# 1248 unused bytes ahead of a second stage's row tiles, with its weight tiles left in place

## The chip, the cores and the metric

The kernel runs on one core of one Trainium2 chip. The metric is the device time of one execution in microseconds (us), the median of several runs; a profiled execution gives the trace from which the rows below are read.

## The reference

The input x has 8 x 3072 rows of 256 float32 numbers. Three steps follow one another; the first two make the kernel's first stage, the last one its second stage.

```python
Y = rfft(x, axis=1) * (filt_r + 1j * filt_i)          # a filter along the 3072 rows
x = irfft(Y, n=3072, axis=1).reshape(24576, 256)
x = maximum(maximum(x @ w1, x @ w2), x @ w3) @ w_out   # 256 -> 768 -> 256
h = x @ w_in2                                          # 256 -> 1024
solu = h * softmax(h)
ln = (solu - mean(solu)) / sqrt(var(solu) + 1e-6) * g_ln
out = ln @ w_out2                                      # 1024 -> 256
```

## The kernel before

Every float32 matrix product is split: an operand is written as a high part and a low part of type float32r (`xh`, `xl`; `wi_h`, `wi_l`), and three of the four products are summed in PSUM.

The first stage holds the filter and the first pair of matrix products. Its matmuls are those of `up` (L713), `down` (L733 to L742) and of the transform (L390). It writes its result to DRAM (`spill`), 512 rows at a time.

The second stage treats 192 tiles of 128 rows. `load2` (L877) brings four tiles from `spill` into `x` and splits them into `xh` and `xl`. `up2` (L886) runs 12 matmuls of 512 columns for each tile: a slice of 128 columns of `xh` or `xl` is the stationary operand, and `wi_h` or `wi_l` moves. `soft` (L902) makes the row maximum (VectorE, L905), the exponential (ScalarE, L907), the product (VectorE, L909), the squares (ScalarE, L911), a few numbers per row in `sm` (VectorE, GpSimd) and a transpose in blocks of 32 into `yt` (VectorE, L926). `exchange` (L929) finishes the transpose of four tiles with 16 DMAs from `yt` to `zt`, issued on SP's queue (L935). `split2` (L948) makes `sh` (ScalarE, L959) and `sl` (GpSimd, L960) from `zt`. `down2` (L963) runs 8 matmuls of 512 columns with `sh` as the stationary operand (L967) and 8 of 256 columns with `sl` (L969); `V2` moves in both. So a tile is 28 matmuls and 20 x 512 + 8 x 256 = 12288 moved columns. The loop at L1018 issues `up2` of tile i, `split2` of tile i - 8 and `down2` of tile i - 9; a planner that runs when the program is built settles the order on each engine. The last four tiles are transposed on TensorE (L945).

In SBUF a pool's buffers lie one behind another in the order in which they are first named, and pools that are opened later lie behind those still open. The waits for memory that another pool used before are made against whole pools. The buffers stand at these byte positions in each partition (a second figure is the second buffer):

```
second stage, weights (pool bp):    wi_h 18432   wi_l 26624   V2 34816
second stage, rows (pool b2):       sh 51200, 55296   x 59392, 63488   xh 67584, 71680
                                    xl 75776, 79872   sl 83968, 88064   (pool ends 92160)
second stage, rows (pools b3, b4):  sm 92160   e 92672   sp 100864   yt 109056, 141824
                                    zt 125440, 158208   oa 174592   ob 176640   (ends 178688)
first stage: df 17376   F 71648   M1 75744   M2 79840   U 101344   yt 118752   zt 122848
             xh 155616   xl 163808   hh and th 176096   hl and tl 182240
             w0h 188384   w0l 200672   ah 212960   woh 217056   wol 223200
```

Pool bp already has a gap of 800 bytes ahead of `wi_h`. All the second stage's large buffers named here start at a multiple of 512 bytes, `wi_h`, `V2`, `sh`, `x`, `xh`, `xl` and `sl` at a multiple of 2048. The first stage's start at 480 bytes past a multiple of 512, thus at 224 past a multiple of 256; its `xh`, `hh`, `hl` and its weights stand 2016 bytes past a multiple of 2048. So in both stages a stationary operand and the operand that moves over it start equally far past a multiple of 512 (only `ones` and `ident`, used in a few float32 matmuls, differ).

The slots of `x` and `xh` also serve `weights2` (L842), which makes the second stage's weights during the last 36 of the first stage's 288 steps, and those of `sh` hold `gw` there.

Of the kernel before, what the change touches and what calls it, by code (L numbers as in the profile page):

```python
# [10 lines left out]
F32 = mybir.dt.float32  # L11
# [8 lines left out]
P = 128  # L20
# [79 lines left out]
def kernel(ctx: ExitStack, tc: tile.TileContext, xr, ff, tw, dft,  # L100
# [727 lines left out]
    wi_l = bp.tile([P, 2, DF2], F32R, tag="wil", name="wil")  # L828
    V2 = bp.tile([P, NF2, 512], F32R, tag="V2", name="V2")
    b2 = ctx.enter_context(tc.tile_pool(name="b2", bufs=2))  # L830
    gwt = [b2.tile([P, 4, D], F32, tag="sh", name=f"gw{j}") for j in range(NF2 // 4)]
    gw = [gwt[c // 4][:, c % 4] for c in range(NF2)]

# [263 lines left out]
```

## Time and profile before

| | |
|---|---|
| median of 3 runs | 2739.02 us (2738.84 to 2740.20) |
| profiled execution, its own time | 2739.05 us |
| profiled execution, span of its instructions | 2737.3 us |
| mean granted clock of TensorE | 0.991 of full speed |
| TensorE busy | 2663.2 us (97%) |
| VectorE, ScalarE, GpSimd busy | 2310.0, 1476.7, 887.6 us |

Times in the rows are microseconds from the start of the span, or nanoseconds where a row gives a mean of one instruction. PE is TensorE's matmuls, PEld its loads of stationary operands, DVE VectorE, ACT ScalarE, POOL GpSimd and SP the SyncE queue. Matmuls overlap in the pipeline, so the length given for one matmul is longer than the distance to the next.

### The profile page before, as it was taken

Reading aid. Unit: us, or ns where it says so; the run is one execution under the profiler, and the core shown is the slowest. Engines: PE = TensorE matmul, PEld = TensorE weight load, DVE = VectorE, ACT = ScalarE, POOL = GpSimd, SP = SyncE. Lnnn points to the kernel's source line nnn. Section 1 sums busy time; section 2 is a strip of 40 time slices with the busy share of each in tenths; the row PEclk is TensorE's granted clock in tenths of the full one; section 3 lists DMA queues with packets and bytes.
Section 4 is the critical chain, followed back from the end, with each engine's and each line's share of the span. In section 5 each row is a group of like instructions: output and inputs, shape, how many; then the busy total and the mean of one; then the engine's idle time right before and its main releaser. Section 6 shows DMA issues by size and latency. Waiting matters only on the chain.

```text
span 2737.3 us, 37911 instructions
## 1 busy us (share of the span) xinstructions
PE 2663.2 (97%) x11992; PEld 2146.3 (78%) x11992; DVE 2310.0 (84%) x4023; ACT 1476.7 (54%) x2883; POOL 887.6 (32%) x1286
## 2 busy tenths in 40 slices
PE   6789999999999999999999999999999999999999
PEld 3467777777777777777777888888888888888888
DVE  8997799999998999999977446888787878788885
ACT  4334444444444444443444335777777777777775
POOL 0000010111101111110102003677767666667765
PEclk9889999999999999999999999999999999999999
DMA  4222123224223223232224112555555555555543
GB/s 165 74 81 94 38 80 104 62 75 127 58 72 117 73 71 111 74 93 69 79 66 125 40 30 81 154 139 146 147 143 144 148 148 141 139 141 144 145 127 90
DMA packets 160745, 284.53 MB, mean 104 GB/s; under 512 B 33952, under 2 KB 93856, under 8 KB 158624
## 3 DMA queue, kind: packets, MB, share of 16 engines
q1 hardware_dynamic: 119840, 231.77, 31.8%
q10 hardware_dynamic: 40704, 50.35, 5.6%
q8 instruction: 94, 1.54, 0.2%
q14 instruction: 107, 0.88, 0.1%
HBM read 89.04 MB, written 50.33 MB: 51 GB/s over the span
## 4 chain that ended last, share of the span: by engine, by line
PE 82%; DVE 13%; DMA 2%; issue 1%; SPq 1%; ACT 1%; POOL 0%; DVEq 0%; ACTq 0%; POOLq 0%
PE h L713 22%; PE h L898 19%; PE p L967 13%; PE p L969 7%; PE pf L390 5%; PE o L742 4%; PE o L734 4%; PE o L735 4%; PE o L733 4%; DVE scr L240 3%; DVE S L244 2%; DVE S L240 1%; DVE M L240 1%; DVE h L718 1%; DVE hl L722 1%
## 5 line engine op out<-in xcount | busy, mean ns | idle before, releaser
L960 POOL TENSOR_TENSOR sl<-zt,sh 128x1024 fp32r<-128x1024 f32 x188 | 452.5, 2407 | 106.2 <-ACT sh L959 99.1
L967 PE MATMUL p<-V,sh 128*128 128x512 f32 x1536 | 380.9, 389 | 0.0
L909 DVE SCALAR_TENSOR_TENSOR sp<-h,e 128x1024 f32<-128x1024 f32 x192 | 234.3, 1220 | 171.8 <-ACT e L907 169.8
L240 POOL TENSOR_TENSOR M<-M,M 128x384 f32<-128x384 f32 (+1 forms) x96 | 135.1, 1428 | 655.1 <-DVE M L240 530.5
L967 PEld LDWEIGHTS p<-V,sh 128*128 128x128 f32 x1536 | 287.4, 188 | 59.5
L721 ACT CAST hh<-h 128x512 fp32r<-128x512 f32 x288 | 169.4, 589 | 286.6 <-DVE h L718 272.7
L716 ACT ACTIVATE hm<-h 128x512 f32<-128x512 f32 x288 | 173.0, 601 | 277.6 <-PE h L713 275.5
L907 ACT ACTIVATE e<-h,sm 128x1024 f32<-128x1024 f32 x192 | 213.7, 1113 | 107.1 <-DVE sm L905 61.2
L959 ACT CAST sh<-zt 128x1024 fp32r<-128x1024 f32 x188 | 196.6, 1047 | 117.9 <-PE p L967 94.9
L905 DVE TENSOR_REDUCE sm<-h 128x1 f32<-128x1024 f32 x192 | 231.1, 1204 | 28.0 <-PE h L898 27.3
L911 ACT ACTIVATE e<-sp,sm 128x1024 f32<-128x1024 f32 x192 | 220.5, 1148 | 55.3 <-DVE sm L913 54.2
L734 PE MATMUL o<-hl,woh 128*128 128x512 f32 x576 | 239.4, 416 | 6.1 <-DVE hl L722 5.9
L898 PE MATMUL h<-wih,x2h 128*128 128x512 f32 x768 | 243.9, 392 | 1.2 <-ACT xo L745 1.2
L898 PE MATMUL h<-wih,x2l 128*128 128x512 f32 x768 | 241.8, 391 | 0.0
L718 DVE TENSOR_TENSOR h<-hm,h 128x512 f32<-128x512 f32 x288 | 198.3, 688 | 49.2 <-PE h L713 46.3
L898 PE MATMUL h<-wil,x2h 128*128 128x512 f32 x768 | 238.0, 390 | 0.0
L926 DVE STREAM_TRANSPOSE yt<-sp 128x1024 f32<-128x1024 f32 x188 | 231.6, 1232 | 5.2 <-DMA zt<-yt 1.0
L733 PE MATMUL o<-hh,woh 128*128 128x512 f32 x576 | 230.7, 400 | 2.9 <-ACT hh L721 2.9
L735 PE MATMUL o<-hh,wol 128*128 128x512 f32 x576 | 228.9, 397 | 0.0
L722 DVE TENSOR_TENSOR hl<-h,hh 128x512 fp32r<-128x512 f32 x288 | 196.7, 684 | 36.4 <-ACT hh L721 36.2
L969 PEld LDWEIGHTS p<-V,sl 128*128 128x128 f32 x1536 | 209.7, 190 | 15.1
L969 PE MATMUL p<-V,sl 128*128 128x256 f32 x1536 | 214.7, 282 | 0.0
(160 smaller groups left out, 5722.3 us busy)
## 6 DMA issues: line engine op xcount, KB each, us to landing
zt<-yt SPq DMA_DIRECT2D x752, 128.0 KB, 2.6
x<-xo SPq DMA_DIRECT2D x96, 256.0 KB, 2.2
x<-x ACTq DMA_DIRECT2D x48, 512.0 KB, 3.6
out_dram<-ob ACTq DMA_DIRECT2D x192, 128.0 KB, 2.3
S<-in_xr_dram SPq DMA_DIRECT2D x15, 1536.0 KB, 7.5
zt<-yt SPq DMA_DIRECT2D x720, 32.0 KB, 1.9
F<-in_ff_dram SPq DMA_DIRECT2D x48, 384.0 KB, 3.4
F<-in_ff_dram SPq DMA_DIRECT2D x16, 512.0 KB, 4.1
```

Source lines behind the costliest of these rows:

```text
L240: eng.tensor_tensor(o, a, b, op=op)
L713: nc.tensor.matmul(ph[j], wt[:, c, f * P:(f + 1) * P], xt[:, c], start=i == 0, stop=i == 5)
L733: nc.tensor.matmul(po[m], wo_h[:, f, cs], hh, start=f == 0, stop=False)
L734: nc.tensor.matmul(po[m], wo_h[:, f, cs], hl, start=False, stop=False)
L735: nc.tensor.matmul(po[m], wo_l[:, f, cs], hh, start=False, stop=False)
L898: nc.tensor.matmul(h[:, fs], xt[:, c, ts], wt[:, c, fs], start=n == 0, stop=n == 5)
L905: nc.vector.tensor_reduce(sm[:, 0:1], h, axis=AX.X, op=ALU.max, negate=True)
L909: nc.vector.scalar_tensor_tensor(sp, h, 1.0, e, op0=ALU.mult, op1=ALU.mult, accum_out=sm[:, 2:3])
L926: nc.vector.transpose(out=YT[g][:, :, t].rearrange("p j c k -> p c j k"), in_=sp.rearrange("p (c j k) -> p c j k", c=NF2, j=4))
L960: nc.gpsimd.tensor_tensor(lv, z, hv, op=ALU.subtract)
L967: nc.tensor.matmul(p, sh[:, c], V2[:, c], start=c == 0, stop=False)
L969: nc.tensor.matmul(p[:, :D], sl[:, c], V2[:, c, :D], start=False, stop=c == NF2 - 1)
```

## The change

One tile of 312 float32 numbers per partition (1248 bytes) is named first in pool b2. Nothing writes or reads it.

```diff
     b2 = ctx.enter_context(tc.tile_pool(name="b2", bufs=2))
+
+    b2.tile([P, 312], F32, tag="gap", name="gap2", bufs=1)
     gwt = [b2.tile([P, 4, D], F32, tag="sh", name=f"gw{j}") for j in range(NF2 // 4)]
```

Every buffer of pool b2 then starts 1248 bytes higher, and so do those of b3 and b4, which lie behind it: `sh` at 52448, `xh` at 68832, `yt` at 110304. The buffers of bp, of the first stage and of PSUM keep their places. 1248 is 2 x 512 + 224, and a multiple of 32.

## Rows read from the trace of the kernel before

**Rows 1.** The page: busy us, share of the span and instructions of each engine.

```profile
PE 2663.2 (97%) x11992; PEld 2146.3 (78%) x11992; DVE 2310.0 (84%) x4023; ACT 1476.7 (54%) x2883; POOL 887.6 (32%) x1286
```

**Rows 2.** Busy time by stretch: columns PE, PEld, DVE, ACT, POOL, clock, DMA.

```profile
300.00:1400.00 1100.00, 1086.67 (x4529) 849.07 (x4528) 1039.50 (x1707) 492.90 (x1186) 134.86 (x106) 1.00 0.29 83
1850.00:2650.00 800.00, 800.00 (x4066) 683.46 (x4065) 643.48 (x1197) 576.01 (x910) 560.01 (x875) 1.00 0.55 143
```

**Rows 3.** The chain that ended last, second stage: start, length, instructions.

```profile
2015.64 2.75 PE h L898 x12
2018.39 1.81 PE p L967 x8
2020.20 0.95 PE p L969 x8
```

**Rows 4.** Costliest groups, second stage from 1900 to 2600 us, shapes kept apart.

```profile
L960 POOL TENSOR_TENSOR sl<-zt,sh 128x1024 fp32r<-128x1024 f32 x127 | 305.6, 2406 | 61.3 <-ACT sh L959 59.3 <-issue 2.0
L967 PE MATMUL p<-V,sh 128*128 128x512 f32 x1016 | 251.1, 389 | 0.0
...
L959 ACT CAST sh<-zt 128x1024 fp32r<-128x1024 f32 x128 | 133.9, 1046 | 75.8 <-PE p L967 66.1 <-POOL sm L916 9.1
...
L240 DVE TENSOR_TENSOR x2l<-x,x2h 128x1024 fp32r<-128x1024 f32 x32 | 38.5, 1203 | 0.0
```

**Rows 5.** The chain that ended last, first stage.

```profile
506.31 2.75 PE h L713 x12
...
525.56 2.72 PE o L742 x12
```

**Rows 6.** The chain again, where the first stage's stationary th and tl are used.

```profile
173.58 0.12 PE h L214
173.69 0.12 PE h L215
```

**Rows 7.** Groups of ScalarE, first stage from 300 to 1400 us.

```profile
L721 ACT CAST hh<-h 128x512 fp32r<-128x512 f32 x205 | 120.7, 590 | 182.1 <-DVE h L718 180.8 <-PE o L735 1.2
```

**Rows 8.** Groups of VectorE in the same stretch.

```profile
L722 DVE TENSOR_TENSOR hl<-h,hh 128x512 fp32r<-128x512 f32 x205 | 139.7, 683 | 8.4 <-ACT hh L721 8.3
```

**Rows 9.** Groups of GpSimd over the whole span.

```profile
L240 POOL TENSOR_TENSOR M<-M,M 128x512 f32<-128x512 f32 x24 | 34.0, 1437 | 202.1 <-DVE M L240 135.5 <-ACT T L560 19.1 <-ACT hh L721 17.9
...
L849 POOL TENSOR_TENSOR wil<-we,wih 128x512 fp32r<-128x512 f32 x4 | 5.1, 1297 | 0.0
```

**Rows 10.** DMA issues, first stage: KB each, median us from issue to landing.

```profile
F<-in_ff_dram SPq DMA_DIRECT2D x13, 512.0 KB, 4.1
```

**Rows 11.** DMA queues and issues, second stage.

```profile
q1 hardware_dynamic: 27924, 76.32, 40.5%
...
zt<-yt SPq DMA_DIRECT2D x585, 128.0 KB, 2.6
...
x<-x ACTq DMA_DIRECT2D x35, 512.0 KB, 3.6
```

**Rows 12.** SP's queue from 2000 to 2016 us, in order of time.

```profile
2004.83 10.04 SPq L935 DMA_DIRECT2D zt<-yt  x16
```

**Rows 13.** ScalarE from 2000 to 2024 us, in order of time.

```profile
2014.78 1.05 ACT L959 CAST sh<-zt 128x1024 fp32r<-128x1024 f32 x1 [1.65 <-PE p L967]
...
2020.53 1.03 ACT L959 CAST sh<-zt 128x1024 fp32r<-128x1024 f32 x1
```

**Rows 14.** Waits from 1900 to 2600 us: in total, times, longest.

```profile
DVE yt L926 <- DMA zt<-yt: 1.0, 2, 0.5
```

**Rows 15.** Busy time by stretch where one stage gives way to the other.

```profile
1400.00:1600.00 200.00, 198.30 (x868) 162.14 (x866) 122.32 (x206) 81.90 (x153) 23.70 (x22) 1.00 0.23 70
1600.00:1800.00 200.00, 198.84 (x944) 166.57 (x943) 137.05 (x246) 118.20 (x193) 83.98 (x151) 1.00 0.38 101
```

**Rows 16.** The chain at a transform's matmuls, 384 columns of float32.

```profile
529.87 1.29 PE pf L390 x4
```

**Rows 17.** Matmuls of one line, second stage: length min, median, max in ns.

```profile
L898 PE MATMUL h<-wih,x2h x582: 389/389/398, 1850.1 to 2649.7; 128*128 128x512 f32 x194
```

## The prediction

> **What bounds the kernel now.** I read the page first: TensorE is busy 97% of the span, VectorE 84% [rows 1]. The table by stretch then separates the stages [rows 2]. From 1850 to 2650 us, where only the second stage runs, TensorE is busy 800.00 of 800.00 us at the full granted clock, while VectorE, ScalarE and GpSimd are busy 643, 576 and 560 us. The chain that ended last shows the same thing as a beat [rows 3]: 12 matmuls of `up2` in 2.75 us, 8 of `down2` with `sh` in 1.81, 8 with `sl` in 0.95, and the next tile follows at once. One tile is 5.51 us, and 192 tiles are 192 x 5.51 = 1058 us. So the second stage costs what its matmuls cost, and an edit there shows in the time only in two ways: the distance from matmul to matmul changes, or another engine or a transfer comes so late that TensorE has to wait. The first stage keeps all its addresses and its operations.
>
> **The change part by part.** No instruction is added, taken out or reshaped; the unused tile has no reader and no writer. What changes is where the operands lie, so I ask of each kind of operation whether the trace holds the same kind at an address like the new one. It does, because the first stage's buffers start 224 bytes past a multiple of 256, and 1248 is also 224 past a multiple of 256. The first stage is therefore a sample of the new position, as far as position within 256 bytes goes.
>
> *Matmuls with row tiles as stationary operand.* In the first stage, operands at that position take 2.75 us for 12 (`up`) and 2.72 us for 12 (the product with `ah`) [rows 5], 0.227 to 0.229 us each. The second stage's, at multiples of 512, take 1.81 / 8 = 0.226 and 2.75 / 12 = 0.229 [rows 3]. Narrow ones, where a load of 128 columns has the least time to hide, go 0.12 us apart in the first stage with `th` and `tl` as stationary operand [rows 6], and 0.95 / 8 = 0.119 in the second [rows 3]. The distance is thus the same at both positions: 0 per matmul for the position of the stationary operand by itself. What no row shows is a float32r matmul whose stationary and moving operands start at different distances past a multiple of 512; all pairs of both stages are alike in this, and afterwards the second stage's differ by 224. Against an effect speaks that within the second stage the slices lie 0, 512, 1024 and 1536 bytes past a multiple of 2048, against moving operands that lie at 0, and yet a matmul's length stays between 389 and 398 ns [rows 17]. I take 0 for this too, and bound it by 9 ns (398 - 389) on the losing side and by the whole surplus per matmul on the winning side. That surplus: 12288 columns at 2.4 GHz are 5.120 us, the tile takes 5.51, so (5.51 - 5.12) / 28 = 14 ns per matmul.
>
> *ScalarE, VectorE and GpSimd on the moved buffers.* ScalarE's cast takes 590 ns for 512 elements at the first stage's position and 1046 for 1024 at the second's [rows 7, 4]; less a fixed part (2 x 590 - 1046 = 134) that is 456 for each further 512, one rate. VectorE's subtraction takes 683 for 512 and 1203 for 1024 [rows 8, 4]; fixed part 163, rate equal again. GpSimd's two-input operation takes 1437 ns for 512 at the first stage's position and 1297 at the aligned one [rows 9], so at worst 11% more. Eleven per cent of `sl`'s 2406 ns [rows 4] is 0.26 us per tile. The room is larger: GpSimd is busy 560 of 800 us [rows 2], 3.86 of each 5.51, leaving 1.65 us; VectorE 4.43, leaving 1.08; ScalarE 3.97, leaving 1.54. Without that room the 0.26 us would cost 192 x 0.26 = 50 us. The distances among these moved buffers stay as they were, since they all move together. Cost 0, with no range of its own.
>
> *Transfers.* The exchange of four tiles issues 16 DMAs over 10.04 us, from 2004.83 to 2014.87 [rows 12]; with 2.6 us to land [rows 11] the last is there at about 2017.5. The cast that can first use them is the one at 2020.53, since the one at 2014.78 began before the last issue was over [rows 13]; the margin is 3.0 us. VectorE waits for an exchange to have left `yt` for only 1.0 us in 700 [rows 14]. A price for the new position: 512 KB into `F`, at the first stage's position, lands in 4.1 us, and 512 KB into `x`, aligned, in 3.6 [rows 10, 11]. That is 14% at most, as other things differ too. On 2.6 us it is 0.36, inside the 3.0. The large queue's share of the DMA engines would go from 40.5% [rows 11] to 46%, still far from full. Cost 0; if the cover were gone, 0.36 us for each of 47 exchanges, 17 us.
>
> The Trainium skill has a rule that speaks against the change here. Its page "DMA: Bandwidth & Descriptors", section "How a descriptor splits into AXI transactions", says that a packet that doesn't start at a multiple of 256 bytes has its first transaction fetched from the boundary below. By it a 4096-byte packet that starts at 224 would take 8 + 15 x 8 + 7 = 135 beats in place of 128, an estimate of 5.5% more, which is less than the 14% allowed for above. By either the sum is the same, as 3.0 us cover it.
>
> *Order and memory reuse.* `weights2` uses the same slots, 1248 bytes higher. Pool b2 would end at 93408, still inside the first stage's pool that ends at 101344 (where `U` begins), and b3 and b4 still lie over the same pools, so the waits for freed memory are against the same work. The planner should put out the same order. Where the stages meet, TensorE is idle (200 - 198.30) + (200 - 198.84) = 2.9 us in 400 [rows 15]; if a wait there vanished or doubled, that is -2.9 or +2.9 us.
>
> **The sum.** 2737.3 us of span, plus 0 for each part, plus the 1.75 us that lie around the span in the profiled execution (2739.05). The profiled execution lies 0.03 us from the median of the three runs (2739.02), so 2739.0 us.
>
> **Rivals.**
>
> *Slower: the two operands of a matmul get in each other's way.* The stationary operand of the next matmul is read while the present one's operand still moves. If the new distance of 224 bytes makes these reads collide, the distance between matmuls grows, and as TensorE is never idle in this stage it decides from the first nanosecond. Price by the only lengthening of a wide matmul that the trace shows, 9 ns [rows 17]: 20 wide matmuls x 192 tiles x 9 ns = 34.6 us, 2773.6 us. For it: this distance is untried in float32r. Against: the even lengths over four other distances. 15%, with whatever other loss is left out above.
>
> *Faster: the same reads collide now.* A float32 matmul of the transform has far less surplus: 1.29 / 4 = 322.5 ns for 384 columns [rows 16], which is twice 160 ns (384 at 2.4 GHz) plus 2.5 ns. If the float32r surplus of 14 ns came from operands that start alike, and fell to 2.5, the gain would be 11.5 x 28 x 192 = 61.8 us, 2677 us. For it: the surplus is there in both stages, and in both the operands start alike. Against: it is the same at all four slices, so a quarter of the distances tried should have shown something else. 9%.
>
> The Trainium skill, page "TensorE: Matmul & The Clock Gate", section "Back-to-back issue gap", gives N / 2.4 + 2.5 ns for a lone stream. The float32 row agrees with it and the float32r rows don't; by the rule for all 28 a tile would take 5.19 us, the time of this rival.
>
> *No change for another reason: GpSimd slows and is hidden.* `sl` is written in runs of 32 elements that would no longer begin at a multiple of 128 bytes. GpSimd would decide only if `sl` took 1.65 us more, 4.06 in place of 2.41, a growth of 69%; the rows show 11% at most. The time would be 2739, so this goes with the forecast. The same holds for a slower exchange up to 3.0 us.
>
> **How the numbers follow.** No change: 76%, of which a few parts in the hundred belong to small shifts where the stages meet. Slower 15%, faster 9%. A measurement of this kernel can tell about 0.2% (5.5 us) from no change. The range goes down to 2733, the forecast less twice the 2.9 us where the stages meet, and up to 2774, the slower rival at its bound. What is left out is the faster rival and a loss beyond 9 ns per wide matmul, together about 12 in 100. In the likeliest case alone I expect 2733 to 2745.
>
> **What would show it.** In the changed kernel's chain the three rows of a tile should again read 2.75, 1.81 and 0.95 us, and TensorE should be busy all of the 800 us from 1850 to 2650. If 1.81 becomes 1.88 or more, or the lengths of L898's matmuls spread above 398 ns, the slower rival holds; if it falls towards 1.73, the faster one. `sl`'s mean tells of GpSimd, the 2.6 us to landing of the DMAs. The prediction is wrong if the distance between matmuls depends on how the two operands lie to one another, or if the planner puts the work into another order.

## The result and the profile after

The changed kernel takes 2755.77 us (median of 3 runs, 2754.55 to 2756.17) against 2739.02: a ratio of 1.0059, 95% interval 1.0036 to 1.0082. Its profiled span is 2754.0 us, 16.7 more than before. The instructions stand in the same order on every engine; in the changed kernel the lines behind the edit have numbers two higher, so L900, L969 and L971 are the L898, L967 and L969 of before.

The table by stretch of the changed kernel (columns as in [rows 2]):

```profile
1850.00:2650.00 800.00, 800.00 (x4001) 668.97 (x4000) 634.49 (x1178) 566.51 (x893) 546.40 (x860) 1.00 0.57 142
300.00:1400.00 1100.00, 1086.47 (x4527) 848.73 (x4527) 1039.55 (x1706) 493.08 (x1185) 132.81 (x106) 1.00 0.29 83
```

In the first stage hardly anything moved: 4527 matmuls in the 1100 us, 4529 before [rows 2]. In the second TensorE is still busy for the whole of its 800 us and still at the full clock, but gets 4001 matmuls done in place of 4066. At 28 a tile that is 800 x 28 / 4001 = 5.60 us per tile against 800 x 28 / 4066 = 5.51, 0.09 more, and 192 x 0.09 = 17 us. So the whole loss is in the distance from matmul to matmul; no engine waits for anything new. The chain of one tile says where it sits (the answer to [rows 3]):

```profile
2021.23 2.80 PE h L900 x12
2024.03 1.87 PE p L969 x8
2025.90 0.93 PE p L971 x8
```

The 12 matmuls of `up2` take 2.80 us in place of 2.75, the 8 with `sh` 1.87 in place of 1.81, and the 8 narrow ones with `sl` 0.93 in place of 0.95. Wide ones lost, narrow ones won a little. The groups (as in [rows 4], here with the narrow matmuls):

```profile
L962 POOL TENSOR_TENSOR sl<-zt,sh 128x1024 fp32r<-128x1024 f32 x126 | 303.5, 2409 | 71.0 <-ACT sh L961 70.8 <-issue 0.2
L969 PE MATMUL p<-V,sh 128*128 128x512 f32 x1000 | 253.5, 395 | 0.0
...
L971 PE MATMUL p<-V,sl 128*128 128x256 f32 x1000 | 137.1, 279 | 0.0
...
L961 ACT CAST sh<-zt 128x1024 fp32r<-128x1024 f32 x125 | 130.7, 1046 | 82.8 <-PE p L969 54.6 <-POOL sm L916 26.3 <-POOL sm L918 1.5
...
L240 DVE TENSOR_TENSOR x2l<-x,x2h 128x1024 fp32r<-128x1024 f32 x31 | 37.3, 1202 | 0.0
```

The lengths of a matmul with `sh` went from 389 to 395 ns, while GpSimd's `sl` (2409 for 2406), ScalarE's cast (1046 for 1046) and VectorE's `x2l` (1202 for 1203) are what they were [rows 4]. The lengths of `up2`'s matmuls (as in [rows 17]: minimum, median, maximum):

```profile
L900 PE MATMUL h<-wih,x2h x571: 393/396/397, 1853.0 to 2649.9; 128*128 128x512 f32 x191
```

Before, the same line had 389/389/398. Not a single one of these 571 is as short as the usual one was, and none is longer than the longest was. The transfers (as in [rows 11] and [rows 14]):

```profile
q1 hardware_dynamic: 27648, 75.53, 41.8%
...
zt<-yt SPq DMA_DIRECT2D x576, 128.0 KB, 2.8
```

```profile
DVE yt L928 <- DMA zt<-yt: 1.0, 2, 0.5
```

An exchange lands in 2.8 us where it landed in 2.6, and VectorE's wait for it is 1.0 us in 700, as before: covered.

### The profile page after: what moved, and what is told of

The parts are those of the page before. It is cut to its first block, busy times and chain, and to the rows that moved or that the text cites. A ratio compares the mean times of both kernels' runs of the same rounds, so it can differ in the third digit from the quotient of the medians.

```text
span 2754.0 us, 37911 instructions
## 1 busy us (share of the span) xinstructions
PE 2679.8 (97%) x11992; PEld 2141.2 (78%) x11992; DVE 2313.3 (84%) x4023; ACT 1478.8 (54%) x2883; POOL 881.1 (32%) x1286
## 4 chain that ended last, share of the span: by engine, by line
PE 80%; DVE 13%; SPq 2%; DMA 2%; issue 2%; ACT 1%; POOL 1%; DVEq 0%; ACTq 0%; POOLq 0%
PE h L713 20%; PE h L900 20%; PE p L969 13%; PE p L971 7%; PE pf L390 6%; PE o L742 3%; PE o L734 3%; PE o L735 3%; PE o L733 3%; DVE scr L240 3%; SPq L678 2%; DVE S L244 2%; DVE S L240 1%; DVE h L718 1%; DVE M L240 1%
## 5 line engine op out<-in xcount | busy, mean ns | idle before, releaser
L962 POOL TENSOR_TENSOR sl<-zt,sh 128x1024 fp32r<-128x1024 f32 x188 | 452.9, 2409 | 122.4 <-ACT sh L961 117.5
L969 PE MATMUL p<-V,sh 128*128 128x512 f32 x1536 | 390.4, 395 | 0.0
L969 PEld LDWEIGHTS p<-V,sh 128*128 128x128 f32 x1536 | 286.9, 187 | 69.2
L961 ACT CAST sh<-zt 128x1024 fp32r<-128x1024 f32 x188 | 196.5, 1046 | 129.8 <-PE p L969 81.5
L900 PE MATMUL h<-wih,x2h 128*128 128x512 f32 x768 | 246.5, 395 | 1.2 <-ACT xo L745 1.2
L900 PE MATMUL h<-wih,x2l 128*128 128x512 f32 x768 | 245.1, 395 | 0.0
L900 PE MATMUL h<-wil,x2h 128*128 128x512 f32 x768 | 241.7, 395 | 0.0
L971 PEld LDWEIGHTS p<-V,sl 128*128 128x128 f32 x1536 | 207.1, 188 | 17.7
L971 PE MATMUL p<-V,sl 128*128 128x256 f32 x1536 | 211.2, 279 | 0.0
```

Source lines behind the costliest of these rows:

```text
L900: nc.tensor.matmul(h[:, fs], xt[:, c, ts], wt[:, c, fs], start=n == 0, stop=n == 5)
L962: nc.gpsimd.tensor_tensor(lv, z, hv, op=ALU.subtract)
L969: nc.tensor.matmul(p, sh[:, c], V2[:, c], start=c == 0, stop=False)
L971: nc.tensor.matmul(p[:, :D], sl[:, c], V2[:, c, :D], start=False, stop=c == NF2 - 1)
```

## The experiments

The theory that the profile after suggests: the pace of a float32r matmul depends on how far apart its two operands start, counted past some round number, since TensorE reads the stationary operand of the next matmul while the present one's moving operand still streams. The first rival: the row tiles' own position, 224 past a multiple of 256, sets the pace. The second: the buffers of the other engines and of the DMAs, which moved too, disturb TensorE's reads. In every kernel below TensorE's instructions stand in the same order as before.

**Weights and rows moved together**, so that their distance is as before:

```diff
-    bp.tile([P, 200], F32, tag="gap", name="gap")
+    bp.tile([P, 512], F32, tag="gap", name="gap")
```

> The gap in pool bp grows from 800 to 2048 bytes and there is none in b2: weights and row tiles both lie 1248 bytes higher, so the moving and the stationary operand again start equally far past a multiple of 512. Theory (the distance between the two operands sets the pace): as before, 2739 us, with 1.81 us for 8 matmuls with sh and 0.95 for 8 with sl. Rival (the row tiles' own position, 224 past a multiple of 256, sets it): 2756 us, with 1.87 and 0.93. Second rival (the moved buffers of the other engines and the DMAs disturb TensorE's reads): 2756 us.

Measured: 2738.32 us, ratio 0.9998 (0.9989 to 1.0007). The row tiles, the moving weights and all other buffers lie where the first rival and the second want them to do harm, and the chain is that of before:

```profile
2021.09 2.75 PE h L898 x12
2023.84 1.81 PE p L967 x8
2025.65 0.95 PE p L969 x8
```

**A distance made from the other side**, by moving the weights and leaving the rows on their old grid:

```diff
-    bp.tile([P, 200], F32, tag="gap", name="gap")
+    bp.tile([P, 512], F32, tag="gap", name="gap")
...
-    b2 = ctx.enter_context(tc.tile_pool(name="b2", bufs=2))
+    b2 = ctx.enter_context(tc.tile_pool(name="b2", bufs=2)); b2.tile([P, 200], F32, tag="gap", name="gap2", bufs=1)
```

> The weights lie 1248 bytes higher and the row tiles 2048 (gaps of 2048 bytes in bp and 800 in b2): row tiles are at multiples of 2048 as before, but 800 bytes past the weights' grid, 288 past a multiple of 512. Theory (distance): slower than before, near 2756 us, with 1.87 us for 8 matmuls with sh. Rival (the row tiles' own position): 2739 us, 1.81. Second rival (other engines' buffers, here on their old grid): 2739 us.

Measured: 2757.59 us, ratio 1.0068 (1.0055 to 1.0080), and in the chain the wide matmuls are those of the changed kernel though every row tile is at a multiple of 2048 (the narrow ones stay at 0.95):

```profile
2022.06 2.80 PE h L898 x12
2024.86 1.87 PE p L967 x8
2026.73 0.95 PE p L969 x8
```

These two settle it against both rivals: neither place by itself matters, their distance does.

**Only the other engines' buffers moved:**

```diff
-            PB[2] = ctx.enter_context(tc.tile_pool(name="b3", bufs=2))
+            PB[2] = ctx.enter_context(tc.tile_pool(name="b3", bufs=2)); PB[2].tile([P, 312], F32, tag="gap", name="gap3", bufs=1)
```

> The 1248 bytes stand at the start of b3: sh, x, xh, xl and sl keep their places, and only sm, e, sp, yt, zt, oa and ob move. Theory and rival alike: 2739 us with 1.81 and 0.95. Second rival (the moved buffers of other engines and DMAs): 2756 us with 1.87 and 0.93.

Measured: 2739.39 us, ratio 1.0002 (0.9993 to 1.0011). `yt`, `zt`, `e` and `sp` at their new places cost nothing:

```profile
2017.13 2.75 PE h L898 x12
2019.88 1.81 PE p L967 x8
2021.69 0.95 PE p L969 x8
```

The transfers do notice the move. The large queue (packets, MB, share of the DMA engines, as in [rows 11]), here and in the kernel with a gap of 256 bytes that follows below, where `yt` and `zt` lie at multiples of 256:

```profile
q1 hardware_dynamic: 27840, 76.08, 42.3%
```

```profile
q1 hardware_dynamic: 27859, 76.14, 40.3%
```

That is 5% more time per packet, and TensorE does not wait for it.

**`sh` left in place, the other row tiles moved:**

```diff
-    gw = [gwt[c // 4][:, c % 4] for c in range(NF2)]
+    gw = [gwt[c // 4][:, c % 4] for c in range(NF2)]; b2.tile([P, 312], F32, tag="gap", name="gap2", bufs=1)
```

> The 1248 bytes stand behind the two buffers of sh, so sh keeps its place and x, xh, xl, sl and all of b3 and b4 move. Theory and rival alike (each matmul's own two operands): 8 matmuls with sh take 1.81 us again, 12 of up2 2.80 and 8 with sl 0.93 as in the changed kernel, so 192 x (5.54 - 5.51) = 6 us over before, 2745 us. Second rival (other engines' buffers and DMAs): all three rows as in the changed kernel, 2756 us.

Measured: 2749.45 us, ratio 1.0038 (1.0025 to 1.0051): 10 us over before where 6 were expected. The chain shows why:

```profile
2016.29 1.82 PE p L967 x8
2018.11 0.94 PE p L969 x8
2019.05 2.80 PE h L898 x12
2021.85 1.85 PE p L967 x8
```

`up2` and `sl` are as in the changed kernel, but the 8 with `sh`, whose operands are at their old distance, take 1.82 us in one tile and 1.85 in the next, not 1.81 in all. In the starts of the records the 8 go 226 to 227 ns apart where 11, 13 or 21 matmuls of `up2` stand ahead of them, but 236, 224, 231, 236, 228, 233, 231 where 12 do. So a matmul's pace depends on those just before it as well. It also depends on the next one: from the last matmul with `sh` to the first with `sl` it is 235 ns in every tile, 227 before, though the one that streams then has both its operands in their old places and only the next one's stationary operand has moved. That part of the expectation, each pair by itself, was wrong by 4 us.

**How far is far?** Four gaps in place of the 1248 bytes, of 64, 32, 16 and 8 float32 numbers:

```diff
-    b2.tile([P, 312], F32, tag="gap", name="gap2", bufs=1)
+    b2.tile([P, 64], F32, tag="gap", name="gap2", bufs=1)
```

> Gap of 256 bytes in place of 1248, all else as in the changed kernel: row tiles 256 past the weights' grid of 512. Theory (the two reads keep step only when the distance is a multiple of 512, the width of one stationary slice): near 2756 us, 1.87 us for 8 matmuls with sh. Rival (only the place inside a shorter line counts, 256 bytes or less): 2739 us, 1.81.

> Gap of 128 bytes. Theory (multiples of 512 alone): near 2756 us, 1.87. Rival (a line of 128 bytes or less): 2739 us, 1.81. A line of 256 bytes: slow here, not at 256.

> Gap of 64 bytes. Theory (multiples of 512 alone): near 2756 us, 1.87. Rival (a line of 64 bytes or less): 2739 us, 1.81. If the loss grew with the distance, a few us over 2739.

> Gap of 32 bytes, the smallest step at which buffers are placed. Theory (multiples of 512 alone): near 2756 us, 1.87. Rival (a line of 32 bytes or less): 2739 us, 1.81; with a line of 64 this one is slow and the gap of 64 is not.

Measured: 256 bytes 2738.51 us (1.0003, 0.9994 to 1.0012), 128 bytes 2755.15 (1.0065, 1.0048 to 1.0081), 64 bytes 2753.13 (1.0057, 1.0042 to 1.0072), 32 bytes 2757.19 (1.0073, 1.0058 to 1.0088). So a distance of 256 bytes is as good as none, which the multiples of 512 of my theory didn't allow, and a line of 128 bytes or less falls too, as 128 is slow. Nor does the loss grow with the distance; the smallest one costs at least as much as the others. The stretch from 1850 to 2650 us of the gaps of 256, 128, 64 and 32 bytes, one kernel after the other:

```profile
1850.00:2650.00 800.00, 800.00 (x4065) 683.55 (x4064) 643.35 (x1199) 576.85 (x908) 560.09 (x874) 1.00 0.55 143
```

```profile
1850.00:2650.00 800.00, 800.00 (x3999) 672.79 (x3998) 634.08 (x1178) 566.09 (x891) 545.51 (x860) 1.00 0.55 142
```

```profile
1850.00:2650.00 800.00, 800.00 (x4011) 670.14 (x4010) 636.37 (x1185) 567.28 (x894) 548.32 (x860) 1.00 0.55 142
```

```profile
1850.00:2650.00 800.00, 800.00 (x3994) 670.88 (x3993) 633.66 (x1175) 565.66 (x891) 544.43 (x860) 1.00 0.55 142
```

The kernel with the weights moved has its rows at 33568 bytes past the weights, 32 past a multiple of 256, and so should be the twin of the gap of 32 bytes:

```profile
1850.00:2650.00 800.00, 800.00 (x3991) 670.74 (x3990) 635.13 (x1178) 564.43 (x890) 545.32 (x858) 1.00 0.54 142
```

It is: 3991 and 3994 matmuls, 1.0068 and 1.0073. As the one distance is 288 past a multiple of 512 and the other 32, what counts repeats after 256 bytes. The 1248 bytes of the change are 224 in this count.

**A further distance**, 192:

```diff
-    b2.tile([P, 312], F32, tag="gap", name="gap2", bufs=1)
+    b2.tile([P, 48], F32, tag="gap", name="gap2", bufs=1)
```

> Gap of 192 bytes in place of 1248, all row tiles of the second stage. Theory (only multiples of 256 keep step): near 2755 us, about 1.87 us for 8 matmuls with sh. Rival (some other distances are good too, and 0 is not special): 2739 us, 1.81.

Measured: 2738.27 us, ratio 1.0000 (0.9990 to 1.0009). The theory that only multiples of 256 keep the time fell here. The stretch, and the chain of a tile:

```profile
1850.00:2650.00 800.00, 800.00 (x4065) 680.27 (x4064) 643.42 (x1200) 575.37 (x909) 561.46 (x875) 1.00 0.56 144
```

```profile
2018.87 2.75 PE h L898 x12
2021.61 1.83 PE p L967 x8
2023.45 0.91 PE p L969 x8
```

It is not the rhythm of before, though: the 8 with `sh` take 1.83 us, 0.02 more, and the 8 with `sl` 0.91, 0.04 less in this tile. Over the stretch the 8 narrow ones gain 8 x 2.7 = 22 ns a tile (116.4 ns apart, 119.1 before) and the 20 wide ones lose about as much. The sum comes out equal.

**The first stage**, its weights left in place and its `xh`, `xl`, `hh` and `hl` 128 bytes lower:

```diff
-    wp = pa.enter_context(tc.tile_pool(name="wp", bufs=1, side="right"))
+    wp = pa.enter_context(tc.tile_pool(name="wp", bufs=1, side="right")); wp.tile([P, 32], F32, tag="gap", name="gap0")
```

> The kernel before with a gap of 128 bytes in the first stage's weight pool, which lies at the top of memory: the first stage's weights stay, its xh, xl, hh, hl, th and tl (and the buffers of yp and zp) lie 128 bytes lower, and the second stage is as before. Theory (any matmul of float32r whose operands differ by other than a multiple of 256): the first stage's 5760 wide matmuls go about 5 ns further apart, as with 128 bytes in the second stage, 29 us more, 2768 us, and 12 of L713 take 2.79 us or more in place of 2.75. Rival (something of the second stage alone, such as its row tiles being the stationary operand): 2739 us, 2.75.

Measured: 2757.36 us, ratio 1.0069 (1.0056 to 1.0083). There the weights are the stationary operand and the rows move, and the same thing happens; the answer to [rows 5]:

```profile
500.50 2.79 PE o L742 x12
...
511.55 2.79 PE h L713 x12
```

12 matmuls of `up` take 2.79 us in place of 2.75, and 12 of the product with `ah` 2.79 in place of 2.72. Over the whole first stage the starts of the records give 227.75 ns from one wide matmul to the next before and 232.51 here (steps under 300 ns, so without pauses), in the pattern that the gap of 128 bytes has in the second stage too (229, 230, 232, 241, 232, 231): 4.76 more, about the 5 ns of the expectation, and 5760 x 4.76 = 27 us. Only 19.4 of them show in the time, because this stage, unlike the second, is not one unbroken stream. The stretch from 300 to 1400 us:

```profile
300.00:1400.00 1100.00, 1088.92 (x4479) 842.50 (x4478) 1032.28 (x1695) 486.30 (x1176) 134.43 (x106) 1.00 0.28 82
```

TensorE is idle for 11.1 us of it, 13.3 before [rows 2], and steps of 300 ns and more from one wide matmul to the next number 188 in the stage in place of 211. Slower matmuls leave less to wait for, and most of the 8 us that don't show went there. So the price per matmul in the expectation was right, and that all of it shows was wrong.

**Can it be turned to use?** With every row tile 64 bytes off, the narrow matmuls went faster (115.4 ns from start to start in the trace, 119.1 before), so `sl` alone was moved, by 64 and by 192 bytes (48 numbers):

```diff
-        sl = b2.tile([P, NF2, P], F32R, tag="sl", name="sl")
+        "gap" in X2 or X2.update(gap=b2.tile([P, 16], F32, tag="gap", name="gap2", bufs=1)); sl = b2.tile([P, NF2, P], F32R, tag="sl", name="sl")
```

> The kernel before with a gap of 64 bytes ahead of sl alone (sh, xh and xl keep their places; b3 and b4 move too, which cost nothing in e4_b3b4). With every row tile 64 bytes off, the narrow matmuls with sl were the one kind that went faster, 115.4 ns apart in place of 119.1. Theory (each pair of operands has its own pace, and the pace carries over by a few matmuls): 8 with sl in 0.92 us in place of 0.95, so 192 x 8 x 3.7 ns = 5.6 us less, 2733 us, if the wide ones that follow settle no more slowly than before. Rival (the wide ones lose their step after such narrow ones, as those with sh partly did in e3_not_sh, where they were 2.5 ns further apart): 192 x 20 x 2.5 = 10 us more, less the 5.6: 2743 us.

> The kernel before with a gap of 192 bytes ahead of sl alone. With every row tile at 192 the narrow matmuls with sl went 116.4 ns apart, against 119.1 before and 117.8 with sl alone at 64, while the wide ones at 192 lost about as much. Theory (each distance has its own pace, so each kind of matmul can be given its best one): 8 with sl in 0.93 us, the wide ones as before, 192 x 8 x 2.7 ns = 4 us less than before, 2734 us. Rival (the pace depends as much on the matmuls around it, so nothing is to be had by one operand alone): 2738 us, with the narrow ones at 119 or the wide ones slower by as much as the narrow ones gain.

Measured: 64 bytes 2735.73 us, ratio 0.9993 (0.9985 to 1.0002); 192 bytes 2740.40 us, 1.0006 (0.9997 to 1.0015). The first may be 2 us better than before but isn't clear of the measurement; the second gains nothing. The chains, 64 and then 192:

```profile
2018.93 2.74 PE h L898 x12
2021.67 1.81 PE p L967 x8
2023.49 0.94 PE p L969 x8
```

```profile
2016.85 2.77 PE h L898 x12
2019.62 1.81 PE p L967 x8
2021.43 0.94 PE p L969 x8
```

Both have 0.94 for the narrow ones; with 192 `up2`, which follows them, pays it back, 2.77 for 2.75. In the starts of the records, wide matmuls whose operands are a multiple of 256 apart come to a steady 226 to 227 ns after the narrow ones: the sixth of them before and with 64, the tenth with 192. At a distance of 224 they never do, but repeat 231, 235, 234, 234; at 128 about half of them alternate between 229 and 238; at 192 they go 226, 229, 232.

## Why the prediction was wrong

It forecast no change, 2739.0 us; it became 16.7 us slower. The range held the time only because the slower rival was priced in, at a price that fitted by luck (below).

- *What bounds the kernel*: right. TensorE stayed busy for 800 of 800 us and the loss shows one to one.
- *ScalarE, VectorE, GpSimd*: right, the three lengths compared above are within 3 ns of [rows 4]. The GpSimd rival, hidden in any case, didn't occur.
- *Transfers*: right that they are covered. They land in 2.8 us, up by 0.2 where 0.36 was allowed, and the large queue's share went to 41.8%, not to the 46% allowed. Per packet that is 4.2% more than before [rows 11], and 4.8% with only the other engines' buffers moved. Where the Trainium skill's "DMA: Bandwidth & Descriptors" ("How a descriptor splits into AXI transactions") gives 5.5%, as an estimate, the queue's time per packet comes near it at 224 bytes; the gap of 128 bytes, also off the 256 grid, shows only 0.8% (40.4% for 27647 packets). The landing times can't tell: with that gap it was 2.6 us, as before.
- *Order and memory reuse*: right. The order is the same, and TensorE is busy 198.31 and 198.84 of 200 us where the stages meet, as in [rows 15].
- *Matmuls, the position by itself*: right. With weights and rows both at 224 past a multiple of 256 the time is as before.
- *Matmuls, the distance between the two operands*: this is the step that failed, the one put as "I take 0 for this too". The evidence for 0 was that slices at 0, 512, 1024 and 1536 bytes all run alike [rows 17]. But these are all multiples of 256, as are all distances of both stages, so the four readings were one reading: the trace of before held no sample of any other distance, and I weighed an untried case by samples that could not differ. The first stage, taken as a sample of the new place, was one of the place alone: there both operands stand at 224, so their distance is a multiple of 256 again. The term, 0, measured 0.09 us per tile.
- *The slower rival*, at 15%, had what decides, the distance between the two operands, and the place and the point from which it counts; that the two reads collide, as it put it, is not shown. Its chance was set by the same four readings. Its price of 9 ns on 20 wide matmuls gave 34.6 us, and that this came within about twice the loss is luck: the lengths of 396 to 398 ns in [rows 17] are those of the first two wide matmuls behind the narrow ones of each tile, so they tell of the order of the matmuls and not of the position of a slice. Measured: (2.80 - 2.75) + (1.87 - 1.81) = 0.11 us per tile on the wide ones, 5.5 ns each, and 0.02 back on the narrow ones, which it did not have. The sign that I named, 1.88 or more for 8 with `sh` or lengths above 398 ns, was set too high: 1.87 and at most 397 were enough.
- *The faster rival* fell: no distance tried brought the wide matmuls below 226 ns in the mean, where it needed 216.

Why the distance between the two operands counts stays open. The Trainium skill speaks against it: its page "SBUF — State Buffer", section "Who interferes with whom", gives TensorE two independent read ports and says that TensorE never waits on anyone. For other engines the runs show nothing against it: moving only their buffers left the time as it was (1.0002). Between TensorE's own two operands they speak against it: 32 bytes of distance cost 0.7%. That the load of the next stationary operand and the stream of the present moving one collide is argued from this and from the 235 ns above, not shown. Distances of 96 and 160 bytes, and those below 32, were not tried.

## What to carry to other kernels

Where TensorE runs float32r matmuls without a pause, keep the start of a stationary slice and the start of what moves over it a multiple of 256 bytes apart, and look at that whenever a small tile is put ahead of large ones: 32 bytes cost as much here as 1248 (192 cost nothing, but the wide matmuls lost there what the narrow ones gained). When a trace shows something to be indifferent, ask how many different cases it really held; readings that agree in the very thing that changes say nothing of it. If the time moves and no engine waits longer, count matmuls in a stretch in which TensorE is never idle.

## What was not expected of the hardware

- Wide float32r matmuls (512 columns) in an unbroken stream settle at 226 to 227 ns from start to start when their operands start a multiple of 256 bytes apart, and go about 233 at distances of 32, 64, 128 or 224; at 192 they average 229.
- Narrow ones (256 columns) go the other way at some distances: 119.1 ns apart at 0, 116.9 at 224, 116.4 at 192, 115.4 at 64; at 32 and 128 they stay near 119 (118.4 and 119.2).
- The pace carries over: after narrow matmuls it takes five to nine wide ones until the steady pace is back, and in some mixes it doesn't come back. Where only the next matmul's stationary operand has moved, the step to it is already longer, 235 ns for 227.
